# GEGLU feed-forward on one core: x's first two blocks and the gate rows in turn on one queue, the table load first on ScalarE, short matmuls without data in the head

## The chip, the core and the metric

The kernel runs on one core of a Trainium2 chip. The metric is the device time of one execution in microseconds (us), the median of several runs. The core has five engines that work side by side, each through its own list of instructions in order: TensorE (PE; its weight loads are shown as PEld), VectorE (DVE), ScalarE (ACT), GpSimd (POOL) and SyncE (SP). Data come from device memory by DMA: an engine, here SyncE or ScalarE, issues a transfer to its queue, and the 16 DMA engines of the core carry it out. The engines keep in step by semaphores.

## The reference

```python
# x: 32 x 32 x 1024 bf16 (1024 rows of 1024), w_gate, w_up: 1024 x 3584, w_down: 3584 x 1024
def reference(x, w_gate, w_up, w_down):
    return (_gelu(x @ w_gate) * (x @ w_up)) @ w_down
```

`_gelu` is the tanh form. All inputs and the output are bf16.

## The kernel before

Both stages (gate and up together, then down) are one level of a Strassen-like scheme with seven products of half-size blocks, whose sums of blocks GpSimd and VectorE make while TensorE multiplies. The contraction of 1024 is eight blocks of 128; `KD` = 4 of them are one half, `KQ` = 2 a quarter. The rows of x are two halves of `NB` = 512. In the names, `a12` is the lower half of W_gate's rows, and `b11`, `b21`, `b12`, `b22` are the four quarters of x transposed (the contraction in the partitions).

Products that need no sum come first. These are the products "ahead": the second half of the contraction of W_gate times `b21`, in groups of four column tiles (`KB` = 4); group `i` reads `a12_ahead[i]`, each a tile of four blocks of 128 rows by 512 columns. They give TensorE work while the rest is loaded and summed.

The order of all instructions stands as it is written: the part under `tc.manual_schedule()` (L195) keeps, on every engine, the order of the code. The head of it, which the change touches, runs as follows.

- x must reach TensorE with the contraction in the partitions. The first two of `b21`'s four blocks are loaded as they are by `load_nat` (L196, tile `x_nat`, 128 KB each) and transposed on TensorE by `transposed(dt)` (L260: four 128 x 128 transposes into two PSUM tiles `tp`, which VectorE copies to `b21`). The other two blocks, and the rest of x, come by transposing DMAs, `load_xT` (L216).
- The gate rows come by `load_ahead(i, k0, k1, eng)` (L209): blocks `k0` to `k1` of group `i`, 128 KB each, on SyncE's queue if no other is given.
- SyncE issues in this order: x's first block (L203), block 0 and block 1 of group 0, the transposing load of `b21`'s blocks 2 and 3, blocks 2 and 3 of group 0 and of group 1, groups 2 and 3 in halves, the first W_up and W_gate columns (`load_w_all`), group 4, the transposing loads of `b11` and `b12`, group 5, that of `b22`.
- ScalarE issues `probe` (L207; 64 elements of W_gate, read by nothing), x's second block (L223), and blocks 0 and 1 of group 1 (L226). Then comes its table load with a Gelu of one column of `ident` (L252).
- TensorE first runs `NWARM` = 6 matmuls on constants (L256, 512 columns each, result unused), then `transposed(0)`, and then this (L326 to L338): for each of the first two blocks and each half of the columns the four products of group 0, 256 columns wide, with `transposed(1)` after the first four; then the first two blocks of group 1, 512 columns wide; then the other two blocks of both groups, each product followed by a copy out of PSUM by ScalarE or VectorE.

```python
        for j in range(KB):
            product_ahead(ps[1][j], 1, j, 0, KQ)
        for i in (0, 1):
            for j in range(KB):
                product_ahead(ps[i][j], i, j, KQ)
                both[j % 2](ahead_at[i * KB + j], ps[i][j])
```

The build adds the semaphores. Every DMA signals its end on one of eight counters, which are given out in turn in the order in which the built program lists the DMAs of both queues. A DMA whose counter was given out before waits, on the engine that issues it, until the earlier DMA with that counter has landed. In the built program of before the order is: probe (counter 0), x's first block (1), x's second block (2), group 0 block 0 (3), group 1 blocks 0 and 1 on ScalarE (4), group 0 block 1 (5), the transposing load (6), group 0 blocks 2 and 3 (7), group 1 blocks 2 and 3 (0, the first to wait), and so on.

Of the kernel before, what the change touches and what calls it, by code (L numbers as in the profile page):

```python
# [8 lines left out]
ACT = mybir.ActivationFunctionType  # L9
# [4 lines left out]
def kernel(  # L14
# [20 lines left out]
    nc = tc.nc  # L35
    P = nc.NUM_PARTITIONS
    fp32 = mybir.dt.float32
    f32r = mybir.dt.float32r
    bf16 = mybir.dt.bfloat16
# [7 lines left out]
    NB = 512  # L47
    assert N == 2 * NB and D == 2 * NB and F % (4 * P) == 0
    DT, FT = D // P, F // P
    KD = DT // 2  # L50
# [4 lines left out]
    KQ = DT // 4  # L55
    HF = FT // 2
    MT = NB // P
    NWARM = 6
    KB = 4
    QF = HF // 2  # L60
    batches = [(0, KB), (KB, QF), (QF, QF + KB), (QF + KB, HF)]
# [2 lines left out]
    wg_r = w_gate.rearrange("(dt dp) f -> dp dt f", dp=P)  # L64
# [8 lines left out]
    xpool = one.enter_context(tc.tile_pool(name="x", bufs=1))  # L73
    ework = one.enter_context(tc.tile_pool(name="ework", bufs=2))
# [32 lines left out]
    def acc(tag):  # L107
        return ps1.tile([P, NB], fp32, name=f"ps{tag}", tag=tag, bufs=BANKS[tag])
# [78 lines left out]
    ones_w = nc.const_aps.tensor(1.0, [P, P], bf16)  # L187
    ones_m = nc.const_aps.tensor(1.0, [P, NB], bf16)
    ident = xpool.tile([P, P], bf16, name="ident")
    make_identity(nc, ident)  # L190
    NB_P = NB // P
# [3 lines left out]
    with tc.manual_schedule():  # L195
        def load_nat(eng, dt, p0, p1):  # L196
            eng.dma_start(  # L197
                out=x_nat[:, p0:p1, dt * P : (dt + 1) * P],
                in_=xf[p0 * P : p1 * P, (KD + dt) * P : (KD + dt + 1) * P].rearrange("(b p) d -> p b d", p=P),
            )  # L200
# [1 line left out]
        assert KQ == 2  # L202
        load_nat(nc.sync, 0, 0, NB_P)  # L203


        probe = xpool.tile([P // 8, KQ, 2], bf16, name="probe")
        nc.scalar.dma_start(out=probe, in_=wg_r[::8, KD : KD + KQ, :2])  # L207

        def load_ahead(i, k0, k1, eng=nc.sync):  # L209
            f0 = i * KB  # L210
            eng.dma_start(
                out=a12_ahead[i][:, k0:k1, :],
                in_=wg_r[:, KD + k0 : KD + k1, f0 * P : (f0 + KB) * P],
            )

        def load_xT(nb, d0, d1):  # L216
            t = ((b11, b12), (b21, b22))[d0 // KD][nb]
            nc.sync.dma_start_transpose(
                out=t[:, d0 % KD : (d1 - 1) % KD + 1, :], in_=xf[nb * NB : (nb + 1) * NB, d0 * P : d1 * P]
            )  # L220

        load_ahead(0, 0, 1)
        load_nat(nc.scalar, 1, 0, NB_P)  # L223
        load_ahead(0, 1, 2)
        load_xT(0, KD + KQ, DT)
        load_ahead(1, 0, KQ, nc.scalar)  # L226
        a12_ahead += [spool.tile([P, KD, KB * P], bf16, name="a12b", tag=t) for t in ("s2", "s4", "s1", "s3")]
        for i in (0, 1):
            load_ahead(i, KQ, KD)
# [13 lines left out]
        for which in (1, 0):  # L243
            load_w_all(1, which)

        def gelu(src, tag, bufs):
            h = ework.tile([P, NB], bf16, name=tag, tag=tag, bufs=bufs)[:, : src.shape[-1]]
            nc.scalar.activation(h, src, ACT.Gelu_apprx_tanh)  # L248
            return h


        gelu(ident[:, :1], "h0", 6)  # L252

        warm_ps = acc("A")
        for _ in range(NWARM):
            nc.tensor.matmul(warm_ps, lhsT=ones_w, rhs=ones_m, start=True, stop=True)  # L256

        tps = [[ps1.tile([P, HALF * P], bf16, name="tp", tag="A", bufs=BANKS["A"]) for _ in range(2)] for _ in range(KQ)]

        def transposed(dt):  # L260
            for half, tp in enumerate(tps[dt]):
                p0 = half * HALF
                for b in range(HALF):
                    nc.tensor.transpose(  # L264
                        tp[:, b * P : (b + 1) * P], x_nat[:, p0 + b, dt * P : (dt + 1) * P], ident
                    )
                nc.vector.tensor_copy(b21[:, dt, p0 * P : (p0 + HALF) * P], tp)

        transposed(0)

        def prod(ps, lhs, rhs, start):
            for k in range(KD):
                nc.tensor.matmul(  # L273
                    ps,
                    lhsT=lhs[:, k, :],
                    rhs=rhs[:, k, :],
                    start=(start and k == 0),
                    stop=(k == KD - 1),
                    skip_group_check=True,
                )  # L280
# [30 lines left out]
        def first_product(ft):  # L311
            psa = acc("A")
            prod(psa, quads(*chunk_of(ft))[0], b11, True)
            if ft < NAHEAD:
                return psa, gelu(added(ahead_at[ft], psa), "h0", 6)
            return psa, snap(psa, "sn1", 4)
# [34 lines left out]
        tt(t2, b22, t1, SUB)  # L351
        group_ahead(5, "CCAA", between=lambda: nc.scalar.copy(b22r, b22))
        begun = {ft: (psa, gelu(c, "h0", 6)) for ft, (psa, c) in begun.items()}
        tt(t3, b22, b12, SUB)
        next(chunk0)
# [8 lines left out]
        for ci in range(NCH):  # L364
# [8 lines left out]
            sn5, sn2, h1, h0 = [], [], [], []  # L373
# [17 lines left out]
            if fts[-1] < NAHEAD:  # L391
                h0 = first
# [226 lines left out]
```

## Time and profile before

| | us |
|---|---|
| median of 3 runs | 273.55 (273.33 to 275.83) |
| span of the profiled execution | 272.0 |
| TensorE busy | 267.1 (98%) |
| VectorE, GpSimd, ScalarE busy | 201.2, 119.3, 116.1 |
| first matmul on data (L264) | 3.30 |
| first product (L284) | 4.31 |
| last matmul ends | 269.1 |

Three more lines of the timeline show ScalarE in the head (start, length, engine, line, operation; "q" is an engine's DMA issue):

```profile
0.73 0.45 ACTq L207 DMA_DIRECT2D probe<-in_w_gate_dram  x1
2.29 1.28 ACT L248 ACT_TABLE_LOAD   x1 [2.29 <-issue]
3.59 0.21 ACT L248 ACTIVATE h<-ident 128x1 bf16<-128x1 bf16 x1
```

In such a line the time after "idle" in brackets is how long the engine had nothing to do before the instruction, and the arrow names what ended that. A DMA's row gives the issue; its landing is told by the list of DMA issues, as us from the issue. Times within the profile are counted from the span's start. The granted TensorE clock of the profile is 1.00 in all slices, so that the pace of the array is read from the distance of equal matmuls.

### The profile page before, as it was taken

To read this page: it belongs to the slowest core of one execution; us is meant where nothing else is said; L and a number is where in the kernel's file an instruction comes from. 1 tells how busy PE (TensorE), PEld (TensorE's weight loads), DVE (VectorE), ACT (ScalarE), POOL (GpSimd) and SP (SyncE) were. 2 spreads that over 40 slices of the span, in tenths; PEclk is the share of its full clock that TensorE was granted. 3 is DMA by queue.
4 is the path that set the end of the run, shared out by engine and by line. 5 is a ranking of instruction groups with operands and counts; after the bars stand their busy time and mean duration, and the time that the engine had idled before them with its cause. 6 is when DMAs were issued, how large, how long until landed. Compare 5 with 4: busy or idle time off the path is not lost.

```text
span 272.0 us, 3399 instructions
## 1 busy us (share of the span) xinstructions
PE 267.1 (98%) x1199; PEld 193.4 (71%) x1212; DVE 201.2 (74%) x205; ACT 116.1 (43%) x189; POOL 119.3 (44%) x60
## 2 busy tenths in 40 slices
PE   8999999999999999999999999999999999999995
PEld 4444776886787688688688687764458888888884
DVE  1448998886976876876787458569999999997721
ACT  2335865545644643645636535434000307770000
POOL 1090099976995994994995978000000000000000
PEclk9999999999999999999999999999999999999999
DMA  7999130504505505415234290005981437855111
GB/s 174 323 227 281 39 99 17 158 25 130 154 2 154 154 4 154 128 27 157 69 88 118 50 319 17 0 2 182 356 273 60 158 112 253 276 187 174 54 61 58
DMA packets 56048, 35.86 MB, mean 132 GB/s; under 512 B 9824, under 2 KB 56032, under 8 KB 56032
## 3 DMA queue, kind: packets, MB, share of 16 engines
q1 hardware_dynamic: 52736, 33.17, 42.6%
q10 hardware_dynamic: 3296, 2.49, 2.9%
q8 instruction: 9, 0.15, 0.2%
q14 instruction: 7, 0.06, 0.1%
HBM read 31.72 MB, written 2.10 MB: 124 GB/s over the span
## 4 chain that ended last, share of the span: by engine, by line
PE 97%; DMA 1%; issue 0%; SPq 0%; DVE 0%
PE psA L273 38%; PE psA L425 24%; PE psC L273 19%; PE psC L425 7%; PE psA L284 5%; PE psC L284 3%; PE psC L588 1%; DMA a12a<-in_w_gate_dram 1%; SPq L197 0%; PE tp L264 0%; DVE o_last L589 0%
## 5 line engine op out<-in xcount | busy, mean ns | idle before, releaser
L273 PE MATMUL psA<-t,s 128*128 128x512 f32 x224 | 57.2, 397 | 0.0
L248 ACT ACTIVATE h<-c 128x512 bf16<-128x512 f32 x56 | 34.6, 631 | 41.6 <-DVE c L303 41.6
L273 PEld LDWEIGHTS psA<-t,s 128*128 128x128 f32 x224 | 42.1, 188 | 9.5
L170 POOL TENSOR_TENSOR s<-wu 128x1024 fp32r<-128x1024 bf16 x13 | 28.8, 2215 | 32.9 <-DMA wu<-in_w_up_dram 27.9
L171 POOL TENSOR_TENSOR s<-s,wg 128x1024 fp32r<-128x1024 f32 x14 | 31.7, 2263 | 15.0 <-DVE s L170 14.0
L173 POOL TENSOR_TENSOR s<-wg,wu 128x1024 fp32r<-128x1024 bf16 x13 | 28.4, 2188 | 0.0
L273 PE MATMUL psA<-b,wg 128*128 128x512 bf16 x119 | 27.8, 379 | 0.6
L273 PE MATMUL psA<-t,a22r 128*128 128x512 f32 x112 | 27.9, 391 | 0.0
L273 PE MATMUL psC<-t,s 128*128 128x512 f32 x112 | 27.9, 391 | 0.0
L273 PE MATMUL psC<-b22r,s 128*128 128x512 f32 x112 | 27.6, 389 | 0.0
L303 DVE TENSOR_TENSOR c<-sn,psA 128x512 f32<-128x512 f32 x32 | 21.8, 682 | 6.7 <-PE psA L273 5.7
L308 ACT COPY sn<-psC 128x512 f32<-128x512 f32 x28 | 16.4, 590 | 20.9 <-PE psC L273 15.2
L273 PEld LDWEIGHTS psC<-t,s 128*128 128x128 f32 x112 | 21.0, 188 | 4.5
L273 PEld LDWEIGHTS psA<-t,a22r 128*128 128x128 f32 x112 | 21.0, 188 | 4.5
L273 PEld LDWEIGHTS psC<-b22r,s 128*128 128x128 f32 x112 | 21.0, 188 | 4.4
L303 DVE TENSOR_TENSOR c<-sn,psC 128x512 f32<-128x512 f32 x28 | 19.2, 688 | 6.5 <-PE psC L273 6.5
L273 PEld LDWEIGHTS <-wg 128*128 128x128 bf16 x128 | 11.8, 98 | 15.3 <-issue 2.4
L172 POOL TENSOR_TENSOR s<-wg,s 128x1024 fp32r<-128x1024 bf16 x10 | 21.6, 2158 | 0.8
L402 DVE TENSOR_TENSOR lo<-c,h 128x512 bf16<-128x512 f32 x14 | 20.4, 1459 | 0.9
L308 ACT COPY sn<-psA 128x512 f32<-128x512 f32 x32 | 18.4, 592 | 6.1 <-PE psA L273 6.0
L303 DVE TENSOR_TENSOR c<-ahead,psA 128x512 f32<-128x512 f32 x24 | 16.4, 687 | 4.0 <-PE psA L273 2.4
L321 DVE TENSOR_TENSOR hi<-h,psA 128x512 bf16<-128x512 bf16 x14 | 9.6, 688 | 12.4 <-PE psA L273 12.4
(85 smaller groups left out, 381.0 us busy)
## 6 DMA issues: line engine op xcount, KB each, us to landing
wu<-in_w_up_dram SPq DMA_DIRECT2D x14, 512.0 KB, 4.0
wdb<-in_w_down_dram SPq DMA_DIRECT2D x12, 512.0 KB, 4.9
wg<-in_w_gate_dram SPq DMA_DIRECT2D x9, 512.0 KB, 5.2
wdb<-in_w_down_dram SPq DMA_DIRECT2D x12, 384.0 KB, 4.5
v<-in_w_down_dram SPq DMA_DIRECT2D x4, 512.0 KB, 6.4
out_dram<-o_sb ACTq DMA_DIRECT2D x15, 128.0 KB, 1.7
wg<-in_w_gate_dram SPq DMA_DIRECT2D x6, 256.0 KB, 4.6
v<-in_w_down_dram SPq DMA_DIRECT2D x4, 384.0 KB, 7.5
```

The costliest lines, as they stand in the source:

```text
L170: yield engs[0].tensor_tensor(s1, a21, a22, ADD)
L171: yield engs[1].tensor_tensor(s2, s1, a11, SUB)
L172: yield engs[2].tensor_tensor(s4, a12, s2, SUB)
L173: yield engs[3].tensor_tensor(s3, a11, a21, SUB)
L248: nc.scalar.activation(h, src, ACT.Gelu_apprx_tanh)
L273: nc.tensor.matmul(ps, lhsT=lhs[:, k, :], rhs=rhs[:, k, :], start=(start and k == 0), stop=(k == KD - 1), skip_group_check=True,)
L284: nc.tensor.matmul(ps[:, cols], lhsT=a12_ahead[i][:, k, j * P : (j + 1) * P], rhs=b21[:, k, cols], start=(k == 0 and not cols.start), stop ...
L303: tt(t, s, ps, ADD)
L308: nc.scalar.copy(t, ps)
L321: tt(g_of(ft)[:, :NB], h0, psa, MUL)
L402: tt(g_of(ft)[:, NB:], added(sn5[fl], psa[fl]), h1[fl], MUL)
L425: nc.tensor.matmul(banks[m], lhsT=lhs(k)[:, m * P : (m + 1) * P], rhs=rhs(k), start=(start and k == 0), stop=(k == HF - 1), skip_group_che ...
```

## The change

x's second block moves from ScalarE's queue to SyncE's, between the first two blocks of gate rows; the probe is gone; `gelu` and its first call, with the table load, stand ahead of ScalarE's one remaining load in the head, blocks 0 and 1 of group 1; the six matmuls on constants become five, and two matmuls of 128 columns follow them and again `transposed(0)`.

```diff
-    NWARM = 6
+    NWARM = 5
+    NFILL = 2
...
         load_nat(nc.sync, 0, 0, NB_P)
 
-
-        probe = xpool.tile([P // 8, KQ, 2], bf16, name="probe")
-        nc.scalar.dma_start(out=probe, in_=wg_r[::8, KD : KD + KQ, :2])
-
...
+        def gelu(src, tag, bufs):
+            h = ework.tile([P, NB], bf16, name=tag, tag=tag, bufs=bufs)[:, : src.shape[-1]]
+            nc.scalar.activation(h, src, ACT.Gelu_apprx_tanh)
+            return h
+
+
+        gelu(ident[:, :1], "h0", 6)
+
         load_ahead(0, 0, 1)
-        load_nat(nc.scalar, 1, 0, NB_P)
+        load_nat(nc.sync, 1, 0, NB_P)
         load_ahead(0, 1, 2)
+        load_ahead(1, 0, KQ, nc.scalar)
         load_xT(0, KD + KQ, DT)
-        load_ahead(1, 0, KQ, nc.scalar)
...
-        def gelu(src, tag, bufs):
-            h = ework.tile([P, NB], bf16, name=tag, tag=tag, bufs=bufs)[:, : src.shape[-1]]
-            nc.scalar.activation(h, src, ACT.Gelu_apprx_tanh)
-            return h
-
-
-        gelu(ident[:, :1], "h0", 6)
-
         warm_ps = acc("A")
         for _ in range(NWARM):
             nc.tensor.matmul(warm_ps, lhsT=ones_w, rhs=ones_m, start=True, stop=True)
+
+        def fill():
+            for _ in range(NFILL):
+                nc.tensor.matmul(warm_ps[:, :P], lhsT=ones_w, rhs=ones_w, start=True, stop=True)
+
+        fill()
...
         transposed(0)
+        fill()
```

In the built program the DMAs stand in this order after the change: x's first block (counter 0), group 0 block 0 (1), x's second block (2), group 0 block 1 (3), the transposing load of `b21` (4), group 0 blocks 2 and 3 (5), group 1 blocks 2 and 3 (6), groups 2 and 3 in halves (7, 0, 1, 2), W_up's columns (3), and then group 1 blocks 0 and 1 on ScalarE (4 again). ScalarE's list begins with the table load, the Gelu of one column, and this DMA.

## The prediction

> **What bounds the kernel now.** I read the page first, then the chain of waits cut to the first 10 us, then the timeline there, then single DMA issues. The page's list of engines:
>
> ```profile
> PE 267.1 (98%) x1199; PEld 193.4 (71%) x1212; DVE 201.2 (74%) x205; ACT 116.1 (43%) x189; POOL 119.3 (44%) x60
> ```
>
> TensorE fills 98% of the 272.0 us. Its busy time in stretches of 10 us is 9.93 to 10.00 from 10 us to 260 us, and the remaining 4.9 us lie at the ends: 0.8 before the first matmul, 0.4 at 4 us, 2.9 behind the last one, 0.8 scattered. So whatever delays TensorE early moves the end by the same amount, and nothing later can give it back. The chain at the start (start, length, piece):
>
> ```profile
> 0.74 0.45 SPq L197
> ...
> 1.25 3.02 DMA a12a<-in_w_gate_dram
> 4.26 0.05 issue
> 4.31 0.61 PE psC L284 x2
> 4.92 0.43 PE psA L284 x2
> 5.35 0.43 PE tp L264 x4
> 5.77 0.32 PE psC L284 x2
> 6.10 0.22 PE psA L284 x2
> ...
> 7.11 1.95 PE psA L284 x10
> ```
>
> The first block of gate rows, second in SyncE's queue, holds TensorE until 4.31; from there TensorE runs without a break. The same 256-column matmul costs 0.21 at 4.92 and 0.11 at 6.10: the array doubles its pace near 5.85. Now the timeline, TensorE and the queues:
>
> ```profile
> 1.73 0.53 ACTq L211 DMA_DIRECT2D a12a<-in_w_gate_dram  x1
> ...
> 2.32 1.34 SPq L218 DMA_TRANSPOSE b<-in_x_dram  x1
> ...
> 3.30 0.62 PE L264 MATMUL tp<-ident,x_nat 128*128 128x128 bf16 x4
> ...
> 4.31 0.61 PE L284 MATMUL psC<-b,a12a 128*128 128x256 bf16 x2 [0.39 <-DMA a12a<-in_w_gate_dram]
> ...
> 6.95 2.11 PE L284 MATMUL psA<-b,a12a 128*128 128x256 bf16 x10
> ```
>
> The last row is two 256-column matmuls and then the eight 512-column ones of L334: `ps[1]`, the first products that read `a12a_ahead[1]`. They begin at 6.95 + 2 x 0.11 = 7.17. Their rows, issued by ScalarE at 1.73, come 4.6 us later, at 6.33, with 0.84 to spare. From the DMA issues of single windows (size, us from issue to landing):
>
> ```profile
> a12a<-in_w_gate_dram ACTq DMA_DIRECT2D x1, 256.0 KB, 4.6
> x_nat<-in_x_dram ACTq DMA_DIRECT2D x1, 128.0 KB, 3.2
> b<-in_x_dram SPq DMA_TRANSPOSE x1, 4.9
> wu<-in_w_up_dram SPq DMA_DIRECT2D x1, 512.0 KB, 3.9
> ```
>
> The third is the transposing load of L218, which lands at 2.32 + 4.9 = 7.2; the fourth is a load of half a megabyte at 59 us that has the DMA engines to itself.
>
> **The change, part by part.** The sum is made in the profiled execution (272.0 us span); the median of the runs is 273.55, 1.55 above it, and I carry the shift over unchanged.
>
> Small parts, each free while its cover stands. The probe has no reader: removing it is 0 (it held ScalarE's queue 0.45 us). The table load goes from 2.29 to about 0.7 and the tiny Gelu ends near 2.2; ScalarE's next work is a copy at 9.52, so 0. Warm-up is 5 x 0.43 + 2 x 0.11 = 2.35 instead of 6 x 0.43 = 2.56 us from 0.78 and ends at 3.13, before x arrives at 3.25: 0. The two fills behind the first transposes take 2 x 0.11 from 3.73 to 3.94, inside the gap that ends at 4.31; VectorE's first copy ends only at 3.75 + 0.29 = 4.04, so they cost 0 even when the gate rows come early (0.2 if the copy could come before them, which it can't).
>
> SyncE's queue: one more issue in front of L218 (x's second block), 0.51 us by its neighbours, so the transposing load is issued at 2.84 and everything behind it half a microsecond later. The first gate rows now share the engines with nothing on ScalarE's queue: they land at 3.75 if they take the 2.5 us of the x block before them, 4.26 if nothing improves; the products then start between 4.05 and 4.31, a gain of 0 to 0.26. x's second block, issued at 1.77, lands between 4.3 (2.5) and 5.0 (3.2), wanted at 4.93: 0 to 0.1 lost. The second gate rows, issued at 2.30, need 3.0 to 4.4: 5.3 to 6.7, wanted at 6.28; I take 5.3, nearer to the quieter row. Later loads are 0.5 late against margins of 2 us and more (t1 on VectorE waits for x at 21.29 and is read at 27.70): 0.
>
> If the array's pace doubled earlier for the filled gap, at most half of the 1.54 us from 4.31 to 5.85 is saved: 0 to 0.77.
>
> The costly part is an added wait. Completions are signalled on eight counters taken in turn, in the order in which the built program lists the DMAs, and a DMA whose counter was used before waits until that one has landed. Before, `load_ahead(1, 0, KQ)` on ScalarE was fifth and waited for nothing. With the tiny Gelu in front of it, the build lists it thirteenth, behind W_up's load; it takes counter 4, and so ScalarE waits there for the fifth, the transposing load of x (L215 now). What stands behind it on ScalarE is the copy of 9.52, which in any case needs the products; what waits for it is TensorE, in order, at `ps[1]`, with `ps[0]`'s second half behind.
>
> When the transposing load lands: issue 2.84 to 4.18. Lowest: 1.65 after its issue ends, as the tiny probe did (0.45 of issue, landed at 2.1), 5.8. Highest: 2.84 + 4.9 = 7.7. In the row of before, 393 KB of ScalarE's x and gate rows moved beside it; 256 KB of those are now out of the way, which at the mean 240 GB/s of the trace's windows from 2 to 5 us is 1.1 us, against an issue 0.5 later: 7.2 + 0.5 - 1.1 = 6.6. By bytes it is earlier: the first 1024 KB, up to its end, had moved at 6.4, and it landed at 7.2, 0.8 behind; the 768 KB that now lead up to its end had moved at 5.2, so 6.0. I take 6.3, the middle.
>
> How long the 256 KB then take: from 3.2 (ScalarE's 128 KB) to 4.6 (the same load before). SyncE's queue is full by then, and half of the engines' time makes 256 KB cost what 512 KB cost alone, 3.9; rows of 1 KB move a little faster (350 against 290 GB/s), so 3.7.
>
> TensorE is let go at 6.3 + 0.05 + 3.7 + 0.05 = 10.1 instead of 7.17: 2.9 us late. The gains above (0 to 1.0) fall into this wait and vanish. Bounds: 5.8 + 3.2 + 0.1 = 9.1, +1.9; 7.7 + 4.6 + 0.1 = 12.4, +5.2. All other loads then have more time than before, so the next late thing is nothing. Forecast: 272.0 + 2.9 = 274.9 span, 273.55 + 2.9 = 276.45.
>
> The idle stretch is about 3.1 us (7.0 to 10.1), up to 3.9 if the head's gains come. No idle time of that kind stands in this trace; the only gap while the pace was still slow is 0.39. If the array returned to its slow pace, the price lies between 0 and half of the 5.07 us (0.78 to 5.85) that it first took to rise: 2.5. I take 0, by the many gaps of 0.05 that cost nothing, though they are far from 3 us, and keep 2.5 for the range. "TensorE: Matmul & The Clock Gate" (the Trainium skill, Part 1) gives windows of about 3.4 us, the full clock after one busy window and the half clock after one idle window, and names itself against gaps beyond that. The rise at 5.85 fits it, a gap of 3.1 us would just stay under one window, and by the page a relapse would cost half of 3.4, an estimate of 1.7 us, making 278.2.
>
> **The rivals.** First, the wait and the relapse: 276.45 + 2.5 = 278.95. For it: the gap is eight times any seen here. Against: none shown. Second, a short wait: the transposing load lands at 5.8 to 6.0, as only 512 KB precede it, and the gate rows need 3.2 to 3.4, so +1.9 to +2.3: 275.65. For it: half the bytes of `wu` come in 3.9. Against: SyncE's issues, one every 0.5 us, keep all engines busy to 17 us. Third, on the other side: the wait is harmless and the head does what the edit's words say. TensorE starts 0.26 earlier and the pace doubles up to 0.77 earlier: 273.55 - 1.0 = 272.5. It decides only if the gate rows land by about 6.2, so the transposing load by 6.2 - 3.2 = 3.0, before its issue is even over (4.18). Only a wait that isn't there on the chip would allow it.
>
> **How the numbers follow.** Wait alone at about 276.45: 0.55. Short wait (275.45 to 275.85): 0.22. Relapse, or a load near its upper bound (277.7 to 279): 0.20. Harmless: 0.03. About 1% is what a measurement of this kernel can tell from no change, and that is 2.74 us, 276.29. Of the first case a little over half lies above it (0.33), the third wholly (0.20): slower 0.53. Within 1%: the rest of the first (0.22), the second (0.22) and the harmless case but for a hundredth: 0.46. Faster 0.01. Range 275.2 to 278.9: from the short wait, less the 0.2 by which the two nearest runs differ, to the relapse; it leaves out the harmless case and the loads near both their upper bounds with a relapse on top.
>
> **What would show it.** After: ScalarE's issue of the gate rows stands at 6 to 7 us, not near 2.3; the chain of waits names them with TensorE idle 2 to 4 us before the 512-column products; 512-column matmuls 0.22 apart behind the gap mean no relapse, 0.43 a relapse; the two fills at 3.7 to 4.0 and a first product near 4.1. I am wrong if that issue stands before 4 us, if TensorE shows no idle time at 7 us, or if the end does not move with it.

## The result, and the profile after

| | before | after |
|---|---|---|
| median of 6 runs, us | 273.94 | 282.01 (281.42 to 284.1) |
| ratio, 95% interval | | 1.029 (1.026 to 1.033) |
| span of the profiled execution | 272.0 | 279.7 |

The change makes the kernel slower by 8 us, 2.9%. (Ratios leave disturbed runs out, so a ratio and the two medians beside it need not agree to the last digit.)

The chain of waits of the changed kernel at the start (start, length, piece):

```profile
2.80 3.70 DMA b<-in_x_dram
6.50 0.02 issue
6.52 6.00 DMA a12a<-in_w_gate_dram
12.52 0.05 issue
12.56 3.60 PE psA L288 x8
16.16 1.41 PE psC L288 x4
```

Where the chain of before ran through TensorE from 4.31 on, it now runs through two transfers, one behind the other: the transposing load of x lands at 6.50, ScalarE's load of the gate rows is issued at 6.52 and takes 6.00 us. The same in the timeline:

```profile
2.03 0.21 ACT L221 ACTIVATE h<-ident 128x1 bf16<-128x1 bf16 x1
...
3.88 0.38 PE L288 MATMUL psC<-b,a12a 128*128 128x256 bf16 x2
...
6.12 0.38 PE L288 MATMUL psA<-b,a12a 128*128 128x256 bf16 x2
6.52 0.44 ACTq L208 DMA_DIRECT2D a12a<-in_w_gate_dram  x1
...
12.56 3.60 PE L288 MATMUL psA<-b,a12a 128*128 128x512 bf16 x8 [6.06 <-DMA a12a<-in_w_gate_dram]
```

ScalarE is done with its Gelu at 2.24 and then stands until 6.52. The first product starts at 3.88 instead of 4.31, and the products of group 0's first two blocks are through by 6.5. Then TensorE stands for 6.06 us. The eight 512-column matmuls of group 1 that follow take 3.60 us, where before they took 1.89 (7.17 to 9.06). Stretches of the same execution show why (stretch, length, then busy time and instructions of the five engines, the granted clock, the DMA share, GB/s):

```profile
6.50:9.90 3.40, 0.00 (x0) 0.00 (x0) 0.00 (x0) 0.00 (x0) 0.00 (x0) 1.00 0.97 312
9.90:10.65 0.75, 0.00 (x0) 0.00 (x0) 0.00 (x0) 0.00 (x0) 0.00 (x0) 0.77 1.01 328
10.65:12.56 1.91, 0.00 (x0) 0.00 (x1) 0.00 (x0) 0.00 (x0) 0.00 (x0) 0.50 1.11 361
12.56:17.10 4.54, 4.54 (x11) 1.64 (x12) 0.00 (x0) 0.05 (x1) 2.11 (x1) 0.50 1.18 265
17.10:20.00 2.90, 2.90 (x15) 1.28 (x14) 2.06 (x3) 1.95 (x4) 2.74 (x3) 1.00 1.11 245
```

The granted clock falls to 0.50 at about 10.3 (a mean of 0.77 is 54% of the stretch at 1.00), 3.8 us into the idle time, and comes back at 17.1. (As in the profile of before, the granted clock reads 1.00 from the start, although equal matmuls there run at half pace until 5.85; it shows the fall, but not the slow pace of the head.) So the 7.7 us of the span are 12.56 - 7.17 = 5.4 of waiting and half of 4.54 = 2.3 of half pace.

### The profile page after: what moved, and what is told of

It reads as the page before. It is cut to its first block, busy times and chain, and to the rows that moved or that the text cites. A ratio compares the mean times of both kernels' runs of the same rounds, so it can differ in the third digit from the quotient of the medians.

```text
span 279.7 us, 3418 instructions
## 1 busy us (share of the span) xinstructions
PE 269.6 (96%) x1215; PEld 193.7 (69%) x1215; DVE 203.2 (73%) x205; ACT 115.8 (41%) x189; POOL 119.2 (43%) x60
## 4 chain that ended last, share of the span: by engine, by line
PE 94%; DMA 3%; SPq 1%; DVE 0%; issue 0%
PE psA L277 37%; PE psA L429 24%; PE psC L277 18%; PE psC L429 7%; PE psA L288 5%; PE psC L288 2%; DMA a12a<-in_w_gate_dram 2%; DMA b<-in_x_dram 1%; PE psC L592 1%; SPq L208 0%; SPq L198 0%; DVE o_last L593 0%
## 5 line engine op out<-in xcount | busy, mean ns | idle before, releaser
L277 PE MATMUL psA<-b,wg 128*128 128x512 bf16 x128 | 29.4, 380 | 0.0
L406 DVE TENSOR_TENSOR lo<-c,h 128x512 bf16<-128x512 f32 x14 | 21.2, 1516 | 0.9
L406 DVE TENSOR_TENSOR hi<-c,h 128x512 bf16<-128x512 f32 x14 | 17.9, 1276 | 0.9
```

Of the source, the lines that this page charges most:

```text
L277: nc.tensor.matmul(ps, lhsT=lhs[:, k, :], rhs=rhs[:, k, :], start=(start and k == 0), stop=(k == KD - 1), skip_group_check=True,)
L406: tt(g_of(ft)[:, NB:], added(sn5[fl], psa[fl]), h1[fl], MUL)
```

## The experiments

Two questions were open. Is the added wait the whole cause, and not x's second block on the other queue or the matmuls? And why did ScalarE's load take 6.0 us, where 3.7 was reckoned?

**Only the place of the table load undone.**

```diff
-        gelu(ident[:, :1], "h0", 6)
         load_ahead(0, 0, 1)
...
         load_ahead(1, 0, KQ, nc.scalar)
+        gelu(ident[:, :1], "h0", 6)
```

> The change with its table load and Gelu put behind ScalarE's gate rows. Theory (the added wait on a counter costs all of the 8 us, by a late landing and by the clock falling back): the gate rows take a fresh counter, are issued near 0.7 us and land before 6; no idle time at 6.5 us, no granted clock of 0.5; 273.9 less the gains of the head, 272.9 to 273.9. Rival (x's second block on SyncE's queue and the shorter warm-up are what is dear): 279 or more.

Ratio 1.0089 (1.0061 to 1.0116), span 274.2: the idle time and the clock of 0.50 are gone, and with them 5.5 of the 7.7 us of span. But it came out above the expected range, for a new reason. Its chain of waits:

```profile
0.74 4.02 DMA x_nat<-in_x_dram
4.76 0.05 issue
4.81 0.61 PE tp L267 x4
5.42 0.21 PE psA L257 x2
5.63 0.54 PE psC L288 x2
```

The gate rows are now ScalarE's first issue, at 0.74, at the same moment as x's first block, and that block takes 4.02 us instead of 2.5. TensorE starts 1.5 us later than before, and its pace doubles only near 9.1.

**Only the table load moved, in the kernel before.**

```diff
...
+        gelu(ident[:, :1], "h0", 6)
...
         load_ahead(1, 0, KQ, nc.scalar)
...
-        gelu(ident[:, :1], "h0", 6)
```

> The kernel before with the table load and Gelu alone moved ahead of ScalarE's gate rows; probe, x's second block and the six warm-up matmuls stay. Theory of the wait: the gate rows are listed fourteenth, take the counter of the transposing load and wait for it; issue at 6 to 7.5 us, landing at 11 to 13, clock back at 0.5 for some 6 us: 281 to 283. Rival (the order of the queues is what is dear): within 1 us of before, 273 to 275.

281.12 (280.53 to 281.99), ratio 1.026 (1.022 to 1.031), span 279.4. ScalarE issues the rows at 6.45, they take 6.2 us, TensorE stands 5.5 us, and the eight products take 3.60 again. The one call (and its definition) moved ahead of the load, with probe, queues and warm-up as before, makes nearly the whole loss.

**TensorE kept busy in the wait.**

```diff
+        for _ in range(27):
+            nc.tensor.matmul(ps[1][0], lhsT=ones_w, rhs=ones_m, start=True, stop=True, skip_group_check=True)
         for j in range(KB):
             product_ahead(ps[1][j], 1, j, 0, KQ)
```

> The change with 27 matmuls of 512 columns on constants in front of the products of group 1, written to the first of their accumulators, which the first product then overwrites: TensorE is busy in the wait. Theory (2.3 of the 7.7 us are the clock's relapse: 4.6 us from 12.56 to 17.2 at half pace): no granted clock under 1.0, gate rows still land near 12.5, time 282.0 - 2.3 = 279.7 (279.2 to 280.2). Rival (the half pace has another cause, such as the loads themselves): 282 as the change, clock of 0.5 still there.

279.97 (279.81 to 280.44), 2.0 below the change; the span is 278.5, 1.2 below. Two stretches of it:

```profile
6.90:13.48 6.58, 6.03 (x29) 2.60 (x28) 0.00 (x0) 0.00 (x0) 0.00 (x0) 1.00 1.07 329
13.48:20.00 6.52, 6.52 (x31) 2.98 (x32) 2.77 (x4) 2.61 (x5) 4.30 (x3) 1.00 1.29 221
```

The clock stays at 1.00, although the rows land even 0.9 later (6.91 + 6.5 = 13.4), so that between the spans keeping busy is worth 1.2 + 0.9 = 2.1. So the half pace came from the idle time.

**The probe back.**

```diff
+        probe = xpool.tile([P // 8, KQ, 2], bf16, name="probe")
+        nc.scalar.dma_start(out=probe, in_=wg_r[::8, KD : KD + KQ, :2])
```

> The change with the probe put back as ScalarE's first instruction; all counters move on by one, so the gate rows still wait for the transposing load. Theory (the gate rows take 6.0 us instead of 3.7 because of what SyncE has queued by 6.5 us): 6.0 from issue to landing again, time 281.4 to 282.6. Rival (the first load on ScalarE's queue pays something extra, which the probe had paid before): 3.5 to 4.5 us, gap of TensorE under 4.5, time 278 to 280.

A single run: 282.95, the load takes 6.8 us. A price of the first load on ScalarE's queue is not seen; with the table load moved alone, where two loads stood ahead on that queue, it took 6.2. The time lies a little above the expected 282.6, with the landing 0.7 later than in the change.

**Another counter.**

```diff
-        load_halves(2)
-        load_halves(3)
+        load_ahead(2, 0, KD)
+        load_ahead(3, 0, KD)
```

> The change with groups 2 and 3 of the gate rows loaded whole instead of in halves: two DMAs fewer are listed ahead of ScalarE's gate rows, which so take counter 2 and wait for x's second block (landed at 4.3) instead of the transposing load. Theory (the wait and what SyncE has queued by then set the landing): issue at 4.3 to 4.6; SyncE has then queued some 0.8 MB that have not moved, against 1.2 MB at 6.5, so 4 to 5 us to landing, 8.5 to 9.5; TensorE idle 2 to 3 us, no granted clock of 0.5; 275.5 to 277. Rival (the load takes 6 us on ScalarE's queue whatever is queued): landing at 10.5, 277.5 to 280.

Ratio 1.016 (1.009 to 1.022), median 278.6, span 276.2. The wait follows the counter: ScalarE now issues right behind the landing of x's second block, at 4.71, and TensorE stands 2.48 us. The landing, 9.5, is as expected; the clock is not, and the median lies above the range of the theory, in that of the rival, whose landing at 10.5 did not come. It falls to 0.50 all the same:

```profile
7.10:9.00 1.90, 0.00 (x0) 0.00 (x0) 0.00 (x0) 0.00 (x0) 0.00 (x0) 1.00 0.98 323
9.00:9.55 0.55, 0.00 (x1) 0.01 (x1) 0.00 (x0) 0.00 (x0) 0.00 (x0) 0.84 1.08 365
9.55:12.20 2.65, 2.65 (x7) 0.98 (x8) 0.00 (x0) 0.00 (x0) 0.00 (x0) 0.50 1.10 353
12.20:13.20 1.00, 1.00 (x5) 0.38 (x4) 0.00 (x0) 0.00 (x0) 0.00 (x0) 0.71 1.19 294
```

A mean of 0.84 puts the fall at 9.37, 2.3 us after the last matmul, and 0.71 the rise at 12.8. The span agrees: 9.55 - 7.17 = 2.4 of waiting and half of 3.2 = 1.6 make 4.0 of the 4.2 us. The four runs differ more than those of the change: spans from 274.3 to 278.3, with a mean clock from 0.998 down to 0.988; in the change it is 0.987 or 0.988 in all six.

**The matmuls alone, and the probe's removal alone**, in the kernel before:

```diff
-    NWARM = 6
+    NWARM = 5
+    NFILL = 2
...
+        fill()
...
         transposed(0)
+        fill()
```

> The kernel before with the matmul part of the change alone: five on constants, and twice two short ones. Theory (they lie in time in which TensorE waits for data; the pace of the array rises at a moment that differs from run to run): 273.2 to 273.9, ratio 1.000 within 0.004. Rival (the filled gap makes the pace rise earlier): 272.5 to 273.0 with 256-column products 0.11 apart from the first.

0.9998 (0.9972 to 1.0025): nothing.

```diff
-        probe = xpool.tile([P // 8, KQ, 2], bf16, name="probe")
-        nc.scalar.dma_start(out=probe, in_=wg_r[::8, KD : KD + KQ, :2])
```

> The kernel before without the probe, nothing else changed. Theory (what ScalarE issues at 0.73 now shares the engines with x's first block; e1 lost by that): x's second block issued at 0.73 instead of 1.21, x's first block lands 0.2 to 0.5 us later than 3.25, the first gate rows about as before; 273.8 to 274.6, ratio 1.000 to 1.004. Rival (the probe was only a burden): gate rows of group 0 land 0.1 to 0.3 earlier, 273.2 to 273.7, ratio under 1.000.

0.9996 (0.9975 to 1.0018), median 273.54: nothing either, so neither side of that expectation shows in the time (the median lies in the rival's range, the interval takes in both); x's first block lands 0.2 later, the first gate rows 0.1 earlier.

**All loads of the head on SyncE's queue**, with the table load first on ScalarE:

```diff
-        load_ahead(1, 0, KQ, nc.scalar)
+        load_ahead(1, 0, KQ)
```

> The change with the gate rows of group 1 issued by SyncE at the place where the change has ScalarE issue them; table load first on ScalarE, which has nothing else to do in the head. Theory (nothing else in the change is dear): the rows are issued at 2.8, land near 6, TensorE does not wait for them; 272.9 to 273.9. Rival (one queue for all loads of the head is too slow): transposing load lands after 8.8 and TensorE waits at the second half of group 0, 274.5 to 276.

1.0019 (0.9995 to 1.0043), median 274.67: not told apart from before, and above the range that the theory gave. Group 1 no longer waits, but the second half of group 0 does, a little, as the rival had it (the transposing load lands at 7.8, though, not after 8.8):

```profile
9.51 1.04 PE L288 MATMUL psC<-b,a12a 128*128 128x512 bf16 x4 [0.40 <-DMA a12a<-in_w_gate_dram]
```

Those rows are issued at 4.66 and take 4.80 us. From 2 to 4.5 us the loads move 209 GB/s here; in kernels in which both engines issue by then they move 226 (before), 268 (the next experiment) and 293 (without the probe). That one engine alone issues too few bytes would fit, but is not shown.

**x's second block on SyncE's queue, gate rows early**: the first experiment with the probe ahead, so that the gate rows go out at 1.22.

```diff
+        probe = xpool.tile([P // 8, KQ, 2], bf16, name="probe")
+        nc.scalar.dma_start(out=probe, in_=wg_r[::8, KD : KD + KQ, :2])
...
-        gelu(ident[:, :1], "h0", 6)
         load_ahead(0, 0, 1)
...
         load_ahead(1, 0, KQ, nc.scalar)
+        gelu(ident[:, :1], "h0", 6)
```

> The change with the probe first, then the gate rows, then the table load on ScalarE; x's second block on SyncE's queue. Theory (e1 lost 2 us because 256 KB issued at 0.74 shared the engines with x's first block, which landed at 4.8 instead of 3.25): the gate rows are issued at 1.2 and x's first block lands at 3.2 to 3.5; 273.5 to 274.5. Rival (x's second block behind gate rows is what is dear): TensorE waits at its second transposes until 5.5 or later, 275 to 276.

1.0038 (1.0009 to 1.0066), median 275.79: x's first transposes start at 3.18, as the theory had it, and the shared start of the first experiment is gone. But the median lies above the theory's range and in the rival's, and no lower than that of the first experiment (275.70, ratio 1.0089), so that the shared start explains at most a part of that loss. What takes its place is some of the rival: TensorE waits 0.56 at the second transposes, until 5.13, and 0.86 for the second half of group 0. With x's second block on SyncE's queue and the gate rows early, the head is slower than before by a few tenths of a per cent; what each of the two costs alone is not shown.

**Few bytes behind the load.**

```diff
-        for i in (0, 1):
-            load_ahead(i, KQ, KD)
+        for i, k0, k1 in ((0, 2, 3), (0, 3, 4), (1, 2, 4)):
+            load_ahead(i, k0, k1)
+        load_xT(0, 0, KD)
...
-        load_xT(0, 0, KD)
```

> The change with the transposing load of b11 moved ahead of the loads of groups 2 and 3, and blocks 2 and 3 of group 0 loaded one by one, so that ScalarE's gate rows are still listed thirteenth and still wait for the first transposing load. From about 5.8 SyncE is held by the issue of b11's load and puts few bytes behind it. Theory (what SyncE has issued and still issues beside it makes ScalarE's 256 KB take 6.0 us): issue near 6.5 as in the change, 3.5 to 4.8 us to landing, TensorE waits 3.5 to 5 us, 279.5 to 281. Rival (a load on ScalarE's queue after an idle time takes 6 us whatever SyncE does): 6.0 us or more, 282 to 283.

The theory failed: 283.68, ratio 1.036 (1.033 to 1.040), above both ranges. Its DMA issues from 5.7 to 6.5:

```profile
a12a<-in_w_gate_dram ACTq DMA_DIRECT2D x1, 256.0 KB, 7.9
b<-in_x_dram SPq DMA_TRANSPOSE x1, 8.8
```

From 5.74 the transposing load takes until 14.5, with the DMA engines at 118 to 144 GB/s from 8 to 11 us, and ScalarE's rows, issued at 6.39, land at 14.3, almost with it. Bytes were the wrong measure. What holds in these runs is another rule: ScalarE's late load lands at about the time at which a load that SyncE issues about then lands. The change itself, issues from 6.45 to 6.6 (SyncE's row is the load issued at 6.3):

```profile
a12b<-in_w_gate_dram SPq DMA_DIRECT2D x1, 256.0 KB, 5.8
a12a<-in_w_gate_dram ACTq DMA_DIRECT2D x1, 256.0 KB, 6.0
```

In the experiment with the other counter the two are issued at 4.71 and 4.73 and take 4.8 and 4.9; with the table load moved alone, issued at 6.45 (ScalarE) and about 6.3 (SyncE), 6.2 and 6.6. So the landings on the two queues go together.

They are not one strict line, though. In the run just shown, with few bytes behind the load, ScalarE's load was issued later than SyncE's and landed 0.2 us earlier, and in the change packets of both queues move side by side. Its DMA queues (packets, MB, share of the 16 engines' time), the first row from 6.52 to 9 us, the other two from 9.4 to 12 us; q1 is SyncE's queue, q10 ScalarE's:

```profile
q1 hardware_dynamic: 788, 0.76, 96.4%
...
q1 hardware_dynamic: 800, 0.65, 75.2%
q10 hardware_dynamic: 268, 0.26, 29.9%
```

The first packet of ScalarE's load moves at about 9.2, the last at about 12.1. So the 6.0 us are 2.7 in which SyncE's loads alone move, 2.9 in which both share the engines, and 0.4 to the landing.

**An empty line.** Eight loads of 64 elements hold SyncE's issue for 3.7 us and bring almost no bytes:

```diff
+        for n in range(8):
+            tiny = xpool.tile([P // 8, KQ, 2], bf16, name=f"tiny{n}")
+            nc.sync.dma_start(out=tiny, in_=wg_r[::8, KD : KD + KQ, :2])
         def load_halves(i):
```

> The change with eight loads of 64 elements on SyncE's queue ahead of the loads of groups 2 and 3: SyncE issues almost no bytes from 5.3 to some 9 us. ScalarE's gate rows are now listed sixteenth and wait for the first of the eight, which should land near 7.3. Theory (loads of both queues are carried out as one line, so that a load of ScalarE lands when a load issued by SyncE at that moment lands; in the change 6.0 us after its issue, beside 5.8 and 6.2): issued near 7.4 behind a line that has almost run dry, it lands 2.8 to 3.6 us later, at 10.2 to 11; TensorE idle 3.8 to 4.6 us; 279.5 to 281, although it is issued 0.9 us later than in the change. Rival (a late load on ScalarE's queue takes 6 us or more by itself): landing after 13, 282.5 to 284.

280.62, ratio 1.024 (1.018 to 1.031), span 278.9. Its chain of waits:

```profile
5.30 3.40 DMA tiny<-in_w_gate_dram
8.71 0.02 issue
8.73 2.92 DMA a12a<-in_w_gate_dram
11.64 0.05 issue
11.69 3.59 PE psA L291 x8
```

2.92 us instead of 6.00 for the same load, issued 2.2 us later and yet landed 0.9 earlier. So the rival, a slow late load on ScalarE's queue whatever SyncE does, falls: what SyncE has ahead of and beside the load makes it slow. Its first packet moves 1.1 us after the issue instead of 2.7, and all its packets move within 1.5 us instead of 2.9. The miss, the issue at 8.73 instead of 7.4 (and with it the landing at 11.64 instead of 10.2 to 11), fits the same rule: the tiny load took 3.40 us and landed at 8.70, and the gate rows that SyncE had issued ahead of it at 4.79 landed at 8.5. At the start of the kernel, the probe took 2.1.

## Why the prediction was wrong

The direction, the added wait and its place were right; two terms of the sum were too small.

- Cover of the small parts: held. Probe and matmuls alone moved nothing (0.9996 and 0.9998). The first gate rows landed at 3.84 (3.75 to 4.26 was said), x's second block at 4.5 (4.3 to 5.0), the second gate rows at 5.45 (5.3). The head did gain about 0.7 us, and it vanished in the wait, as said.
- "No cost" for loads that come half a microsecond later: nearly. With the big wait taken away and x's first block on time, the variants with x on SyncE's queue have ratios of 1.0019, which the noise covers, and 1.0038; in both, TensorE waits for blocks 2 and 3 of group 0, 0.40 and 0.86 us. The margins of "2 us and more" were a wrong reading for this load: in the kernel before it is issued at 3.71, takes 4.2 us, and is read at 8.89, a margin of 1.0.
- The added wait: shown by moving the table load alone, and by the counter that moved the issue from 6.5 to 4.7 when two DMAs fewer stood ahead.
- Landing of the transposing load: 6.50 against 6.3 taken. (The 393 KB in that step are thousands of bytes, 384 KB as the other sizes are counted; the sum used only 256 of them.)
- "How long the 256 KB then take": the step that failed. I gave ScalarE's load half of the engines' time, 3.7 us, with 4.6 as the upper bound. Issued at 6.45 to 6.91 with SyncE's loads ahead of it, it took 6.0 to 6.8, and 2.9 with almost none. In the change it had 30% of the engines' time while it moved, not half, and the 2.7 us before its first packet, against 1.1 with almost nothing ahead, stood in no term. The better rows stood in the trace of before: SyncE's own 256 KB loads issued at 5.3 to 6.4 took 4.7 to 5.3. I had used ScalarE's early rows, which were issued at 1.21 and 1.73, when the engines had moved almost nothing and little was queued. With 5.3 the wait would have come out as 4.5 instead of 2.9 us.
- The relapse: I took 0 and kept 2.5 as a rival of its own, at 0.20 together with late loads. It cost 2.3 in the change (2.1 by the run with TensorE kept busy). The longer wait makes the relapse surer (mean clock 0.987 or 0.988 in all runs of the change, 0.988 to 0.998 in those with the other counter, whose profiled wait is 2.48), so the two belonged in one case: 5.4 + 2.3 = 7.7. "TensorE: Matmul & The Clock Gate" (the Trainium skill, Part 1) names one idle window of about 3.4 us for the relapse, and I let that rule speak for a gap of 3.1. The length agrees with the traces, in which the changes of the clock lie 3.41 us or twice that apart; but the clock fell 3.8 us into the gap in the change and 2.3 us into it with the other counter, at the end of a step of 3.41 us in which TensorE had still worked for 1.1. The measurement decides: a gap of 2.5 us is not safe.

The rivals: the harmless case fell, the short wait fell, and the relapse, with a wait longer than its own, is what happened. No version ran faster than the kernel before; the matmuls alone and the probe's removal alone equal it.

## What to carry to other kernels

Before moving an instruction ahead of a DMA on its engine, read from the built program where that DMA is listed afterwards and whose counter it takes: one place in the code can turn a free issue into a wait for an unrelated transfer. Price a late load by the landing times of loads that the other queue issues at that moment, not by a share of bandwidth. And when TensorE is to wait for 2.5 us or more (the shortest wait here with a fall of the clock was 2.48), add the half pace that may follow it to the same case.

## What the runs showed of the hardware that I had not expected

- Loads that SyncE and ScalarE issue at about the same time land at about the same time, whichever queue they are on: 5.8 and 6.0 us, 4.9 and 4.8, 8.8 and 7.9 from issue to landing; a load of 64 elements took 3.40 us behind others and 2.1 at the start. A load on ScalarE's queue first stands (2.7 us in the change) and then moves side by side with SyncE's. Why it stands is not shown.
- The granted clock fell to 0.50 between 2.3 and 5.4 us after TensorE's last matmul, in six executions (the change and the experiments with the table load alone, the probe back, the other counter, few bytes and the empty line), and came back 3.2 to 5.8 us after work had begun again. The two changes lie 3.41 us apart with the other counter (9.37 and 12.78) and 6.82 to 6.83 in the five others (10.30 and 17.12 in the change; 9.53 and 16.36, 12.25 and 19.08, 11.73 and 18.56, 9.50 and 16.33 in the order above). Counted in steps of 3.41 us, the step that ended with the fall held no matmul in three of the six, and 1.0 to 1.1 us of matmuls in the three where the fall came after 2.3 to 2.4 us; a step with 1.5 or 1.6 us of them (probe back, few bytes) brought no fall. In these six, then, when the clock falls depends on where the gap lies in these steps as well as on its length.
- In heads that are nearly alike, equal matmuls double their pace at quite different moments: about 3.5 us in the change and without the probe, 5.2 with the matmuls alone, 5.85 before, 6.5 with all loads on SyncE's queue. The two fills do not set this moment: with the same fills it also came at 4.9 (few bytes), 5.4 (probe back) and 6.0 (other counter). In the six executions above it lies one or two steps of 3.41 us before the fall of the clock.
